# Two gated linear-attention blocks on one core: x tile 1 first on ScalarE's queue, its transposes behind tile 0's, A's keys of tile 2 before B's, gate column by a full-array matmul

## The chip, the cores and the metric

One core of one Trainium2 chip. The metric is the device time of one execution in microseconds (us), the slowest core's; with one core there is only one. Every execution also has a *span*: the profile's first program instruction to its last. The reported time is longer than the span.

## The reference

x is 2048 x 640, in bfloat16, with 32 heads of 20 columns. Two blocks, A and B, work on the same x with their own weights:

```
qkv = x @ wqkv;  phi(t) = where(t > 0, t + 1, exp(t)) + 1e-6
kv  = sum_s phi(k)[s] v[s]^T          (per head)
z   = sum_s phi(k)[s]
o   = (phi(q) @ kv) / (phi(q) . z + 1e-6)
out = o @ wo
g   = sigmoid((x * gate_w).sum(-1))
result = g * A + (1 - g) * B
```

## The kernel before

The program is recorded as operations, each with its engine, its inputs and outputs. A small scheduler orders them; on TensorE they stay in the order of recording. x is needed transposed (`XT`). Tiles 0 and 1 of x (128 rows each) are loaded plainly and transposed by TensorE against an identity; the other tiles come by transposing DMAs. The keys of a tile are five *key steps*, one per chunk of 128 rows of the weights; a step is a 128x512 and a 128x128 matmul. B's weights carry a 641st column, the gate's.

```python
    bgw = Buf("gw5")
    dma("ACT", "cst", CST[:, :], cap[:, :], 128 * CW * 2, outs=[bcst])
    ld_x("ACT", 1)
    dma("ACT", "gw", GW5[:, :], gate_w.rearrange("(c p) -> c p", p=128), 1280, outs=[bgw])
    for c in range(NC):
        if c == 0:
            ld_x("SP", c)
        ld_wk("SP", "A", c)
    for c in range(NC):
        ld_wk("SP", "B", c)
    for t0, t1 in ((2, 3), (3, 4), (4, 5), (5, 6), (6, 8), (8, 12), (12, 16)):
        xt_dma(t0, t1)
    ...                                                   # cut: the later loads
    def x_tp(t):                                          # cut: three groups of transposes
        ...                                               # each copied out of PSUM by VectorE
    def gate_col():                                       # gate_w as 5 rows of 128 -> a column
        op("PE", lambda e: e.transpose(tv(), GW5[:, :], IDN[0:NC, 0:NC]), 60.0, ...)
        op("DVE", lambda e: e.tensor_copy(WK["B"][:, :, D : D + 1], tv().unsqueeze(2)), ...)
    ...
    warm(4)                                               # warm-ups of 128x512
    warm(1, 2)
    pss = [Buf("k", "ps", 2) for _ in range(2)]
    x_tp(0)
    warm(6, 1)                                            # six warm-ups of 128x128
    k_step("A", 0, 0, pss[0])
    x_tp(1)
    k_step("A", 0, 1, pss[0])
    k_step("A", 1, 0, pss[1])
    k_step("A", 1, 1, pss[1])
    gate_col()
    for c in range(2, NC):
        for t in range(2):
            k_step("A", t, c, pss[t])
    for t in range(2):
        k_post("A", t, pss[t])
    pss = [Buf("k", "ps", 2) for _ in range(2)]
    for c in range(NC):
        for t in range(2):
            k_step("B", t, c, pss[t])                     # B's chunk serves two tiles
    for t in range(2):
        k_post("B", t, pss[t])
    for t in range(2, NT):
        for X in XS:
            k_unit(X, t)
    ...                                                   # cut: everything later, unchanged
```

Of the kernel before, what the change touches and what calls it, by code (L numbers as in the profile page):

```python
# [6 lines left out]
ACT = mybir.ActivationFunctionType  # L7
# [6 lines left out]
NT = 16  # L14
NB = 4
NC = 5
# [56 lines left out]
class Sched:  # L73
# [7 lines left out]
    def op(self, eng, fn, cost, ins=(), outs=(), after=(), prio=None, name="", dma=None):  # L81
        if eng == "ACT" and dma is None:
            after = list(after) + self.consts
        o = Op(eng, fn, cost, list(ins), list(outs), after, len(self.ops) if prio is None else prio, name, dma)
        self.ops.append(o)
        return o
# [171 lines left out]
def body(nc, A_x, A_wqkv, A_wo, B_x, B_wqkv, B_wo, gate_w, out, log=None):  # L258
# [7 lines left out]
    bf, f32 = dt.bfloat16, dt.float32  # L266
    sb = nc.alloc_sbuf_tensor
    XT = sb("XT", [128, NC, S], bf)
# [47 lines left out]
    TTR = sb("TTR", [128, NB, 4, 128], bf)  # L316
    FF = sb("FF", [128, NB, 512], bf)
    CST = sb("CST", [128, CW], bf)
    GW5 = sb("GW5", [NC, 128], bf)
    GE = sb("GE", [128, NT], f32)  # L320
    GG = sb("GG", [128, 2, NT], f32)
    ONE = sb("ONE", [128, 128], bf)
# [2 lines left out]
    PS = nc.alloc_psum_tensor("ps", [128, 8, 512], f32)  # L325


    IDN = sb("IDN", [128, 128], bf)
# [3 lines left out]
    op = sch.op  # L332
# [6 lines left out]
    def dma(q, name, dst, src, nbytes, ins=(), outs=(), after=(), issue=450.0, transpose=False, prio=None):  # L339
        def fn(e):  # L340
            d = dst() if callable(dst) else dst
            with nc.allow_non_contiguous_dma(reason="layout"):
                return e.dma_start(d, src() if callable(src) else src, transpose=transpose)

        o = op(q, fn, 0.0, ins, outs, after, prio=prio, name=name, dma=(issue, nbytes, 95.0 if transpose else 330.0))
        if loading:
            o.behind = chain.get(q)
            chain[q] = o
        return o
# [4 lines left out]
    def act_cost(n):  # L354
        return 190 + 0.833 * n

    def dve1(n):
        return 155 + 1.04 * n

    def dve4(n):  # L360
# [14 lines left out]
    bid = Buf("idn")  # L375
# [6 lines left out]
        ins=[bone],  # L382
        outs=[bid],
        name="idn",
    )
    bxo = Buf("xo")
    op("POOL", lambda e: e.memset(XN[:, :, D : D + 1], 1.0), 200.0, outs=[bxo], name="xones")

    def ld_x(q, t):
        dma(q, "x%d" % t, XN[:, t, 0:D], x[128 * t : 128 * t + 128, :], 163840, outs=[bxn[t]])  # L390

    def ld_wk(q, X, c, after=()):
        dma(q, "wk%s%d" % (X, c), WK[X][:, c, 0:D], wqkv[X][128 * c : 128 * c + 128, D : 2 * D], 163840, outs=[bwk[X, c]], after=after)

    def xt_dma(t0, t1):
        dma(
            "SP",
            "xt%d" % t0,
            XT[:, :, 128 * t0 : 128 * t1],
            x[128 * t0 : 128 * t1, :],  # L400
            (t1 - t0) * 163840,
            outs=bxt[t0:t1],
            issue=(t1 - t0) * 850.0,
            transpose=True,
        )
# [2 lines left out]
        return wqkv[X][:, k * D : k * D + D].rearrange("(c p) f -> p c f", p=128)  # L408

    bgw = Buf("gw5")  # L410
    dma("ACT", "cst", CST[:, :], cap[:, :], 128 * CW * 2, outs=[bcst])
    ld_x("ACT", 1)
    dma("ACT", "gw", GW5[:, :], gate_w.rearrange("(c p) -> c p", p=128), 1280, outs=[bgw])
    for c in range(NC):
        if c == 0:
            ld_x("SP", c)
        ld_wk("SP", "A", c)
    for c in range(NC):
        ld_wk("SP", "B", c)
    for t0, t1 in ((2, 3), (3, 4), (4, 5), (5, 6), (6, 8), (8, 12), (12, 16)):  # L420
        xt_dma(t0, t1)
    dma("SP", "xr", XN[:, 2:NT, 0:D], x[256:S, :].rearrange("(t p) d -> p t d", p=128), 14 * 163840, outs=bxn[2:])
    for X in XS:
# [14 lines left out]
    def warm(n, w=4):  # L438
        for i in range(n):
            op(  # L440
                "PE",
                lambda e: e.matmul(psw(bw, 128 * w), ONE[:, :], ONE[:, :].unsqueeze(1).to_broadcast([128, w, 128]), start=True, stop=True),  # L442
                107.0 * w,
                ins=[bone],
                outs=[bw],
                name="warm",
            )

    def x_tp(t):
        for lo, hi in ((0, 1), (1, 3), (3, 5)):  # L450
            bt = Buf("tp", "ps")
            for c in range(lo, hi):
                op(
                    "PE",
                    lambda e, c=c, lo=lo, bt=bt: e.matmul(  # L455
                        PS[:, bt.slot, 128 * (c - lo) : 128 * (c - lo) + 128],
                        XN[:, t, 128 * c : 128 * c + 128],
                        IDN[:, :],
                        start=True,
                        stop=True,  # L460
                    ),
                    100.0,
                    ins=[bxn[t], bid],
                    outs=[bt],
                    name="tp%d" % t,
                )
            half = Buf("xth")
            op(
                "DVE",
                lambda e, lo=lo, hi=hi, bt=bt: e.tensor_copy(  # L470
                    XT[:, lo:hi, 128 * t : 128 * t + 128],
                    PS[:, bt.slot, 0 : 128 * (hi - lo)].rearrange("p (c s) -> p c s", c=hi - lo),
                ),
                dve1(128 * (hi - lo)),
                ins=[bt],
                outs=[half],
                name="tpc%d" % t,
            )
            bxt[t].parts = getattr(bxt[t], "parts", []) + [half] * (hi - lo)
# [3 lines left out]
    def gate_col():  # L483
        bt = Buf("gwp", "ps")

        def tv():
            return PS[:, bt.slot, :].bitcast(bf)[:, 0:NC]

        op("PE", lambda e: e.transpose(tv(), GW5[:, :], IDN[0:NC, 0:NC]), 60.0, ins=[bgw, bid], outs=[bt], name="gwt")  # L489
        op(  # L490
            "DVE",
            lambda e: e.tensor_copy(WK["B"][:, :, D : D + 1], tv().unsqueeze(2)),
            170.0,
            ins=[bt],
            outs=[bgc],
            name="gwc",
        )
# [4 lines left out]
    def k_step(X, t, c, ps):  # L502
        w = D + 1 if X == "B" else D

        def fn(e):
            a = psw(ps, w)
            l = XT[:, c, 128 * t : 128 * t + 128]
            e.matmul(a[:, 0:512], l, WK[X][:, c, 0:512], start=(c == 0), stop=(c == NC - 1))  # L508
            return e.matmul(a[:, 512:w], l, WK[X][:, c, 512:w], start=(c == 0), stop=(c == NC - 1))  # L509

        xin = [bxt[t].parts[c] if hasattr(bxt[t], "parts") else bxt[t]]
        op(
            "PE",
            fn,
            mm_cost(512) + mm_cost(128),
            ins=xin + [bwk[X, c]] + ([bgc] if X == "B" else []),
            outs=[ps],
            name="k%s%d_%d" % (X, t, c),
        )
# [3 lines left out]
    def k_post(X, t, ps):  # L523
        ek = Buf("ek", "ek")
        ek2 = Buf("ek2")
        pk = Buf("pk%s%d" % (X, t))
        bpk[X, t] = pk
        first = []
        if X == "B":
            b = Buf("ge")  # L530
            bge.append(b)
            op(
                "ACT",
                lambda e: e.activation(GE[:, t : t + 1], psw(ps, D + 1)[:, D : D + 1], ACT.Exp, scale=-1.0),
                200.0,
                ins=[ps],
                outs=[b],
                name="ge",
            )
            first = [b]  # L540
        op("ACT", lambda e: e.activation(EK[:, ek.slot, :], psw(ps, D), ACT.Exp), act_cost(D), ins=[ps] + first, outs=[ek], name="ke")  # L541
        op(
            "DVE",
            lambda e: e.tensor_scalar(EK[:, ek.slot, :], EK[:, ek.slot, :], 1.0, EPS, op0=ALU.min, op1=ALU.add),  # L544
            dve4(D),
            ins=[ek],
            outs=[ek2],
            name="kt",
        )
        op(  # L550
            "DVE",
            lambda e: e.scalar_tensor_tensor(PKt[X][:, t, :], psw(ps, D), 0.0, EK[:, ek.slot, :], op0=ALU.max, op1=ALU.add),  # L552
            dve1(D),
            ins=[ps, ek, ek2],
            outs=[pk],
            name="ks",
        )

    def k_unit(X, t):
        ps = Buf("k", "ps", 2)  # L560
        for c in range(NC):
            k_step(X, t, c, ps)
        k_post(X, t, ps)
# [2 lines left out]
    warm(1, 2)  # L566
    pss = [Buf("k", "ps", 2) for _ in range(2)]
    x_tp(0)
    warm(6, 1)
    k_step("A", 0, 0, pss[0])  # L570
    x_tp(1)
    k_step("A", 0, 1, pss[0])
    k_step("A", 1, 0, pss[1])
    k_step("A", 1, 1, pss[1])
    gate_col()
    for c in range(2, NC):
        for t in range(2):
            k_step("A", t, c, pss[t])
    for t in range(2):
        k_post("A", t, pss[t])  # L580
    pss = [Buf("k", "ps", 2) for _ in range(2)]
    for c in range(NC):
        for t in range(2):
            k_step("B", t, c, pss[t])
    for t in range(2):
        k_post("B", t, pss[t])
    for t in range(2, NT):
        for X in XS:
            k_unit(X, t)

# [490 lines left out]
```

## Time and profile before

| | |
|---|---|
| median of the first 3 executions | 189.27 us (189.26 to 189.87) |
| profiled execution | 189.12 us, span 187.4 us |
| TensorE busy | 184.8 us |

The page of the kernel before: the span, the busy time of each engine (us, share of the span, instructions), and the chain of waits that ended last, by engine.

```profile
span 187.4 us, 3207 instructions
PE 184.8 (99%) x1266; PEld 108.4 (58%) x1266; DVE 136.0 (73%) x263; ACT 94.5 (50%) x168; POOL 0.6 (0%) x7
PE 99%; DVE 0%; issue 0%; DVEq 0%
```

TensorE is the bound: nearly the whole chain is its. Where its idle time lies, a table by stretches shows (start:end, length, then the busy time and instructions of TensorE, weight loads, VectorE, ScalarE and GpSimd, the granted clock, the DMA share, GB/s). The granted clock averages over recorded time alone, and the record starts at 4.37 us, so the 1.00 of the first line says nothing of the time before:

```profile
0.00:8.00 8.00, 7.56 (x46) 4.03 (x47) 2.27 (x8) 2.07 (x3) 0.59 (x7) 1.00 0.87 252
8.00:13.00 5.00, 5.00 (x39) 2.87 (x38) 4.00 (x8) 2.95 (x7) 0.00 (x0) 1.00 0.92 156
13.00:185.00 172.00, 172.00 (x1184) 101.37 (x1182) 129.44 (x247) 89.05 (x159) 0.00 (x0) 1.00 0.41 98
```

From 8 to 185 us TensorE is busy throughout, so inside the span only the head can move. (Busy times merge overlapping matmuls, so a short wait can hide in them; the distances between starts, below, are the finer measure.) The head, in TensorE's part of the timeline of the kernel before (start and length in us, instruction, `x` how many; `[idle before]`). The 128x128 halves of the key steps are left out here and in the later timelines, but for one; `...` stands for left-out lines:

```profile
2.51 0.69 PE L455 MATMUL ps<-IDN,XN 128*128 128x128 bf16 x5
2.99 0.84 PE L442 MATMUL ps<-ONE 128*128 128x128 bf16 x6
3.63 0.63 PE L508 MATMUL ps<-WKW,XT 128*128 128x512 bf16 x1
4.16 0.55 PE L455 MATMUL ps<-IDN,XN 128*128 128x128 bf16 x5
4.75 0.39 PE L508 MATMUL ps<-WKW,XT 128*128 128x512 bf16 x1
...
5.30 0.38 PE L508 MATMUL ps<-WKW,XT 128*128 128x512 bf16 x1
5.52 0.22 PE L509 MATMUL ps<-WKW,XT 128*128 128x128 bf16 x1
5.67 0.17 PE L489 MATMUL ps<-IDN,GW 5*128 5x5 bf16 x1
5.78 0.39 PE L508 MATMUL ps<-WKW,XT 128*128 128x512 bf16 x1
...
6.39 0.39 PE L508 MATMUL ps<-WKW,XT 128*128 128x512 bf16 x1
...
7.49 0.38 PE L508 MATMUL ps<-WKW,XT 128*128 128x512 bf16 x1
...
9.40 0.38 PE L508 MATMUL ps<-WKW,XT 128*128 128x512 bf16 x1
9.67 0.38 PE L508 MATMUL ps<-WKW,XT 128*128 128x512 bf16 x1
9.94 0.38 PE L508 MATMUL ps<-WKW,XT 128*128 128x512 bf16 x1
```

Lengths overlap here, since matmuls are pipelined (0.38 us long, 0.27 apart); read the distances between starts. L455 are the transposes, L442 the warm-ups, L508 the wide half of a key step. Two steps in the steady stream start 0.27 us apart. Across the gate's transpose (5.67) they are 5.30 and 5.78, 0.48 apart: that instruction costs 0.21 us. 7.49 is the eleventh key step, B's first; from there nothing waits.

### The profile page before, as it was taken

The numbers are of one execution on the slowest core, as the hardware profiler recorded it, in microseconds if no ns is written. First come the engines' busy times: TensorE is split into PE (matmuls) and PEld (weight loads), VectorE is DVE, ScalarE is ACT, GpSimd is POOL, SyncE is SP. The second block draws the span as 40 slices with busy tenths as digits, with TensorE's granted clock in tenths as the row PEclk, the third lists the DMA queues.
The fourth block names the chain that finished last, engine by engine and source line by source line (L and its number), as shares of the span: only waits on it lengthen the run. The fifth ranks groups of instructions, "written<-read, shape, count | busy, mean of one in ns | idle before, by whom it ended". The sixth has DMA issues, their size and how long they took to land.

```text
span 187.4 us, 3207 instructions
## 1 busy us (share of the span) xinstructions
PE 184.8 (99%) x1266; PEld 108.4 (58%) x1266; DVE 136.0 (73%) x263; ACT 94.5 (50%) x168; POOL 0.6 (0%) x7
## 2 busy tenths in 40 slices
PE   9999999999999999999999999999999999999995
PEld 5555555555566656655557556655566655555552
DVE  2489888878833546487798999879996999965600
ACT  3265655565554546644684667877624594100012
POOL 1000000000000000000000000000000000000000
PEclk9999999999999999999999999999999999999999
DMA  7989999999001011011501232540015365132322
GB/s 205 279 162 128 183 381 372 365 227 197 9 0 35 0 38 35 0 35 29 93 9 27 60 48 44 125 113 5 0 37 117 32 152 134 40 138 105 137 79 70
DMA packets 36301, 19.89 MB, mean 106 GB/s; under 512 B 25630, under 2 KB 36286, under 8 KB 36286
## 3 DMA queue, kind: packets, MB, share of 16 engines
q1 hardware_dynamic: 35844, 19.48, 42.9%
q8 instruction: 10, 0.16, 0.4%
q10 hardware_dynamic: 442, 0.20, 0.4%
q14 instruction: 5, 0.04, 0.1%
HBM read 9.39 MB, written 2.62 MB: 64 GB/s over the span
## 4 chain that ended last, share of the span: by engine, by line
PE 99%; DVE 0%; issue 0%; DVEq 0%
PE ps L903 23%; PE ps L743 23%; PE ps L508 19%; PE ps L617 18%; PE ps L618 5%; PE ps L509 5%; PE ps L659 2%; PE ps L442 1%; PE ps L697 1%; PE ps L455 1%; PE ps L698 0%; DVE TSB L947 0%; DVE ONE L372 0%; PE ps L489 0%; DVEq L230 0%
## 5 line engine op out<-in xcount | busy, mean ns | idle before, releaser
L508 PE MATMUL ps<-WKW,XT 128*128 128x512 bf16 x160 | 44.2, 381 | 0.0
L760 ACT ACTIVATE EK<-ps 128x512 bf16<-128x512 f32 x40 | 23.9, 598 | 31.6 <-PE ps L743 29.2
L509 PE MATMUL ps<-WKW,XT 128*128 128x128 bf16 (+1 forms) x160 | 35.2, 220 | 0.0
L541 ACT ACTIVATE EK<-ps 128x640 bf16<-128x640 f32 x32 | 22.3, 703 | 11.6 <-PE ps L509 5.7
L508 PEld LDWEIGHTS ps<-WKW,XT 128*128 128x128 bf16 x160 | 15.7, 98 | 18.9 <-DMA WKW<-in_A_wqkv_dram 0.4
L743 PE MATMUL ps<-XT,WQA 128*128 128x512 bf16 x100 | 24.5, 379 | 0.0
L743 PE MATMUL ps<-XT,WQB 128*128 128x512 bf16 x100 | 23.7, 379 | 0.0
L617 PE MATMUL ps<-XN,PKB 128*128 128x512 bf16 x80 | 23.5, 379 | 0.0
L617 PE MATMUL ps<-XN,PKA 128*128 128x512 bf16 x80 | 23.5, 379 | 0.0
L770 DVE TENSOR_SCALAR EK<-EK 128x512 bf16<-128x512 bf16 x40 | 11.6, 291 | 14.9 <-ACT EK L760 14.6
L618 PE MATMUL ps<-XN,PKA 128*128 128x129 bf16 x80 | 17.6, 220 | 0.0
L618 PE MATMUL ps<-XN,PKB 128*128 128x129 bf16 x80 | 17.6, 220 | 0.0
L903 PE MATMUL ps<-WPA,EX 128*128 128x512 bf16 x120 | 17.3, 299 | 0.0
L903 PE MATMUL ps<-WPB,PKA 128*128 128x512 bf16 x120 | 16.5, 299 | 0.0
L743 PEld LDWEIGHTS ps<-XT,WQB 128*128 128x128 bf16 x100 | 11.0, 118 | 8.5
L509 PEld LDWEIGHTS ps<-WKW,XT 128*128 128x128 bf16 x160 | 15.7, 98 | 0.0
L544 DVE TENSOR_SCALAR EK<-EK 128x640 bf16<-128x640 bf16 x32 | 10.4, 325 | 7.2 <-ACT EK L541 6.9
L743 PEld LDWEIGHTS ps<-XT,WQA 128*128 128x128 bf16 x100 | 10.7, 118 | 8.1
L617 PEld LDWEIGHTS ps<-XN,PKA 128*128 128x128 bf16 x80 | 9.4, 117 | 7.9
L617 PEld LDWEIGHTS ps<-XN,PKB 128*128 128x128 bf16 x80 | 9.4, 117 | 7.8
L949 ACT ACTIVATE TSB<-ps 128x640 bf16<-128x640 f32 (+1 forms) x3 | 2.0, 668 | 23.2 <-PE ps L903 23.2
L552 DVE SCALAR_TENSOR_TENSOR PKB<-ps,EK 128x640 bf16<-128x640 f32 x16 | 13.2, 825 | 0.6
(75 smaller groups left out, 240.6 us busy)
## 6 DMA issues: line engine op xcount, KB each, us to landing
out_dram<-TSB SPq DMA_DIRECT2D x15, 160.0 KB, 1.8
XN<-in_A_x_dram SPq DMA_DIRECT2D x1, 2240.0 KB, 8.8
WKW<-in_A_wqkv_dram SPq DMA_DIRECT2D x5, 160.0 KB, 4.1
WKW<-in_B_wqkv_dram SPq DMA_DIRECT2D x5, 160.0 KB, 4.3
WQA<-in_A_wqkv_dram SPq DMA_DIRECT2D x1, 800.0 KB, 10.5
WQB<-in_B_wqkv_dram SPq DMA_DIRECT2D x1, 800.0 KB, 13.2
WVA<-in_A_wqkv_dram SPq DMA_DIRECT2D x1, 800.0 KB, 12.7
WVB<-in_B_wqkv_dram SPq DMA_DIRECT2D x1, 800.0 KB, 14.2
```

The lines of the kernel that those rows point to most:

```text
L508: e.matmul(a[:, 0:512], l, WK[X][:, c, 0:512], start=(c == 0), stop=(c == NC - 1))
L509: return e.matmul(a[:, 512:w], l, WK[X][:, c, 512:w], start=(c == 0), stop=(c == NC - 1))
L541: op("ACT", lambda e: e.activation(EK[:, ek.slot, :], psw(ps, D), ACT.Exp), act_cost(D), ins=[ps] + first, outs=[ek], name="ke")
L544: lambda e: e.tensor_scalar(EK[:, ek.slot, :], EK[:, ek.slot, :], 1.0, EPS, op0=ALU.min, op1=ALU.add),
L552: lambda e: e.scalar_tensor_tensor(PKt[X][:, t, :], psw(ps, D), 0.0, EK[:, ek.slot, :], op0=ALU.max, op1=ALU.add),
L617: e.matmul(a[:, 0:512], l, XN[:, t, 0:512], start=(t == 0), stop=(t == NT - 1))
L618: return e.matmul(a[:, 512 : D + 1], l, XN[:, t, 512 : D + 1], start=(t == 0), stop=(t == NT - 1))
L659: r = e.matmul(PS[0:GR, ps.slot, GR * i : GR * i + GR], WV[X][:, c, lo : lo + GR], gv[:, c, :, lo // 5 : lo // 5 + 24], start=(c == 0), st ...
L743: r = e.matmul(PS[:, ps.slot, :], WQ[X][:, c, g::5], XT[:, c, 512 * b : 512 * b + 512], start=(c == 0), stop=(c == NC - 1),)
L760: lambda e: e.activation(EQ[:, eq.slot, :], PS[:, ps.slot, :], ACT.Exp),
L770: lambda e: e.tensor_scalar(EQ[:, eq.slot, :], EQ[:, eq.slot, :], 1.0, EPS, op0=ALU.min, op1=ALU.add),
L903: r = e.matmul(a[:, l0 - lo : h0 - lo], PQ[X, b][:, g, 128 * (t % 4) : 128 * (t % 4) + 128], WP[X][:, g, l0:h0], start=(X == first and g = ...
```

## The change

The intent is to have the first key steps earlier: tile 1's data is requested first on its queue, its transposes replace idle warm-ups, its copies go to the idle ScalarE. Using A's tile 2 before B gives B's weights more time. The gate's column is made by an ordinary matmul over all 128 rows (123 of them zero) instead of a transpose of 5 rows.

```diff
-    GW5 = sb("GW5", [NC, 128], bf)
+    GWZ = sb("GWZ", [128, 128], bf)
+    zgw = op("POOL", lambda e: e.memset(GWZ[:, :], 0.0), 200.0, name="zgw")
...
+    ld_x("ACT", 1)
+    dma("ACT", "gw", GWZ[0:NC, :], ..., after=[zgw])
     dma("ACT", "cst", CST[:, :], cap[:, :], 128 * CW * 2, outs=[bcst])
-    ld_x("ACT", 1)
-    dma("ACT", "gw", GW5[:, :], ...)
     for c in range(NC):
         if c == 0:
             ld_x("SP", c)
         ld_wk("SP", "A", c)
+    xt_dma(2, 3)
     for c in range(NC):
         ld_wk("SP", "B", c)
-    for t0, t1 in ((2, 3), (3, 4), ...):
+    for t0, t1 in ((3, 4), ...):
...
+                return e.activation(o, i, ACT.Copy) if t else e.tensor_copy(o, i)
-                "DVE",
+                "ACT" if t else "DVE",
...
-        op("PE", lambda e: e.transpose(tv(), GW5[:, :], IDN[0:NC, 0:NC]), 60.0, ...)
+        op("PE", lambda e: e.matmul(tv(), GWZ[:, :], IDN[:, 0:NC], start=True, stop=True), 60.0, ...)
...
     x_tp(0)
-    warm(6, 1)
-    k_step("A", 0, 0, pss[0])
+    warm(1, 1)
     x_tp(1)
-    k_step("A", 0, 1, pss[0])
-    k_step("A", 1, 0, pss[1])
-    k_step("A", 1, 1, pss[1])
+    for c in range(2):
+        for t in range(2):
+            k_step("A", t, c, pss[t])
     gate_col()
...
-    pss = [Buf("k", "ps", 2) for _ in range(2)]
-    for c in range(NC):
-        for t in range(2):
-            k_step("B", t, c, pss[t])
-    for t in range(2):
-        k_post("B", t, pss[t])
-    for t in range(2, NT):
+    k_unit("A", 2)
+    for t in range(3):
+        k_unit("B", t)
+    for t in range(3, NT):
         for X in XS:
             k_unit(X, t)
```

More of the change, by code (lines that the diff above doesn't have):

```diff
@@ L410, in body @@
     bgw = Buf("gw5")
+    ld_x("ACT", 1)
+    dma("ACT", "gw", GWZ[0:NC, :], gate_w.rearrange("(c p) -> c p", p=128), 1280, outs=[bgw], after=[zgw])
     dma("ACT", "cst", CST[:, :], cap[:, :], 128 * CW * 2, outs=[bcst])
-    ld_x("ACT", 1)
-    dma("ACT", "gw", GW5[:, :], gate_w.rearrange("(c p) -> c p", p=128), 1280, outs=[bgw])
     for c in range(NC):
@@ L417, in body @@
         ld_wk("SP", "A", c)
+    xt_dma(2, 3)
     for c in range(NC):
         ld_wk("SP", "B", c)
-    for t0, t1 in ((2, 3), (3, 4), (4, 5), (5, 6), (6, 8), (8, 12), (12, 16)):
+    for t0, t1 in ((3, 4), (4, 5), (5, 6), (6, 8), (8, 12), (12, 16)):
         xt_dma(t0, t1)
@@ L467, in x_tp, with copy @@
             half = Buf("xth")
-            op(
-                "DVE",
-                lambda e, lo=lo, hi=hi, bt=bt: e.tensor_copy(
-                    XT[:, lo:hi, 128 * t : 128 * t + 128],
-                    PS[:, bt.slot, 0 : 128 * (hi - lo)].rearrange("p (c s) -> p c s", c=hi - lo),
-                ),
-                dve1(128 * (hi - lo)),
+            def copy(e, lo=lo, hi=hi, bt=bt):
+                o = XT[:, lo:hi, 128 * t : 128 * t + 128]
+                i = PS[:, bt.slot, 0 : 128 * (hi - lo)].rearrange("p (c s) -> p c s", c=hi - lo)
+                return e.activation(o, i, ACT.Copy) if t else e.tensor_copy(o, i)
+            op(
+                "ACT" if t else "DVE",
+                copy,
+                act_cost(128 * (hi - lo)) if t else dve1(128 * (hi - lo)),
                 ins=[bt],
@@ L486, in tv @@
         def tv():
-            return PS[:, bt.slot, :].bitcast(bf)[:, 0:NC]
-        op("PE", lambda e: e.transpose(tv(), GW5[:, :], IDN[0:NC, 0:NC]), 60.0, ins=[bgw, bid], outs=[bt], name="gwt")
+            return PS[:, bt.slot, 0:NC]
+        op("PE", lambda e: e.matmul(tv(), GWZ[:, :], IDN[:, 0:NC], start=True, stop=True), 60.0, ins=[bgw, bid], outs=[bt], name="gwt")
         op(
```

## The prediction

> **What bounds the kernel now.** TensorE. The page's busy line gives PE 184.8 of 187.4 us, the chain of waits gives PE 99%. The idle rest is mostly the first 0.39 us and about 2.0 us after the last matmul. Nothing in the diff touches that tail, or TensorE's work after the first 13 us, where the timeline shows one key step (128x512 and 128x128) each 0.272 us without gaps. So only the head can move the time.
>
> **The head, before** (timeline and DMA landing records, us). Tile 0's transposes start at 2.51 (x tile 0 lands 2.37); six short warm-up matmuls follow; key step A0,0 starts at 3.63, at the half clock; tile 1's transposes at 4.16 (x tile 1 lands 3.67); the full clock is granted from 4.37. A's weight chunks 0 to 4 land at 3.22, 4.70, 5.50, 6.35, 6.82. Chunk 1 ends a wait before 4.75 and chunk 3 one before 6.39. The gate transpose costs 0.21 us (0.48 instead of 0.27 between two steps). From 6.39 there are no stalls; the eleventh key step (first of B) starts at 7.49.
>
> **What changes.** Removed: five warm-ups (0.107 us each, cold). Moved: tile 1's five transposes in front of A0,0, its three evacuations (0.95 us on VectorE) to ScalarE, which idles from 3.12 to 7.42; estimate 0.3 to 0.4 us each. The gate matmul should fall from 0.21 to about 0.05 us. By work alone, 0.4 us are won before chunk 2.
>
> But chunks 2 and 3 don't come sooner: the 16 engines are about saturated, the bytes ahead of chunk 3 are the same. The Trainium skill ("DMA: Bandwidth & Descriptors", Queues, rings and completion order) says that each DMA engine round-robins between queues; in this trace x tile 1's packets indeed interleave with SyncE's. Issued at 0.13 instead of 0.51, it should land near 2.8, but take share from x tile 0, which I expect at 2.4 to 2.7. A0,0 then starts at 3.6 to 3.8; A0,3 waits for chunk 3 at about 6.3. The gain shrinks to 0.05 to 0.15 us.
>
> **New risk.** The eleventh step is now A's tile 2. Its DMA transpose, queued behind chunk 4 (6.82), should land about 0.66 us later (as behind B's last chunk before): 7.48, needed at 7.40 to 7.45. A stall of 0 to 0.1 us eats most of the gain. B's chunks then land at about 7.9 to 9.6 (0.42 us apart, as before) and are needed at 8.85 to 9.94, now 0.27 instead of 0.54 us apart: enough, with 0.3 us of slack at the last.
>
> **Prediction: 189.15 us, range 188.7 to 189.8.** Faster by over 2%: 0.5%; same: 99%; slower: 0.5%.
>
> **Signs.** Right: PE still about 99%; A0,3 released by a DMA at 6.2 to 6.4; the gate step under 0.1 us; eleventh step at 7.35 to 7.55; nothing different later. Wrong: x tile 0 later than 2.8; a wait of over 0.2 us for tile 2's transpose or a B chunk; idle PE after 13 us.
>
> **What would make it wrong.** The skill ("TensorE: Matmul & The Clock Gate", Part 1) says the clock's activity window is free-running, so the granting moment (4.37 here) may shift between executions; one trace can't show it. If the new wait for x tile 0 leaves TensorE idle long enough to delay the full clock by a window (about 3.4 us by that page), up to 1 us is lost. If chunk 3 lands earlier, up to 0.4 us is gained.

## The result, and the profile after

| | before | after |
|---|---|---|
| median | 189.26 us (188.97 to 189.87, 6 runs) | 188.91 us (188.65 to 189.32, 6 runs) |
| profiled execution: time | 189.12 us | 188.96 us |
| profiled execution: span | 187.38 us | 187.58 us |
| time minus span | 1.74 us | 1.38 us |

The ratio of after to before is 0.9982, with a 95% interval of 0.9963 to 1.0001. A ratio is the mean time of one kernel's fast runs over that of the other's of the same rounds, so it is not quite the ratio of the medians.

The gain, about 0.35 us, fell within the predicted range. But the span of the profiled execution did not shrink; it grew by 0.2 us. The page of the changed kernel:

```profile
span 187.6 us, 3202 instructions
PE 184.6 (98%) x1261; PEld 107.9 (58%) x1261; DVE 135.4 (72%) x260; ACT 95.6 (51%) x171; POOL 0.8 (0%) x8
PE 96%; DMA 2%; SPq 0%; DVE 0%; issue 0%; DVEq 0%
```

The chain has 2% of DMA now. The stretches of the changed kernel, as above, show TensorE less busy in the first 8 us, and 37 instead of 39 matmuls in the next 5, though it is busy throughout:

```profile
0.00:8.00 8.00, 7.17 (x42) 3.77 (x43) 1.31 (x5) 3.08 (x7) 0.78 (x8) 1.00 0.86 222
8.00:13.00 5.00, 5.00 (x37) 2.56 (x35) 4.45 (x9) 3.03 (x6) 0.00 (x0) 1.00 0.92 195
13.00:185.00 172.00, 172.00 (x1182) 101.31 (x1180) 129.31 (x246) 88.92 (x158) 0.00 (x0) 1.00 0.39 99
```

The head in TensorE's timeline of the changed kernel (L457 are the transposes, L513 the wide half of a key step, L494 the gate):

```profile
2.64 0.69 PE L457 MATMUL ps<-IDN,XN 128*128 128x128 bf16 x5
3.12 0.31 PE L444 MATMUL ps<-ONE 128*128 128x128 bf16 x1
3.23 0.74 PE L457 MATMUL ps<-IDN,XN 128*128 128x128 bf16 x5
3.76 0.63 PE L513 MATMUL ps<-WKW,XT 128*128 128x512 bf16 x1
4.30 0.44 PE L513 MATMUL ps<-WKW,XT 128*128 128x512 bf16 x1
5.09 0.39 PE L513 MATMUL ps<-WKW,XT 128*128 128x512 bf16 x1 [0.30 <-DMA WKW<-in_A_wqkv_dram]
5.37 0.38 PE L513 MATMUL ps<-WKW,XT 128*128 128x512 bf16 x1
5.64 0.17 PE L494 MATMUL ps<-IDN,GWZ 128*128 128x5 bf16 x1
5.70 0.39 PE L513 MATMUL ps<-WKW,XT 128*128 128x512 bf16 x1
...
7.39 0.39 PE L513 MATMUL ps<-WKW,XT 128*128 128x512 bf16 x1
...
9.30 0.38 PE L513 MATMUL ps<-WKW,XT 128*128 128x512 bf16 x1
9.70 0.39 PE L513 MATMUL ps<-WKW,XT 128*128 128x512 bf16 x1
10.12 0.39 PE L513 MATMUL ps<-WKW,XT 128*128 128x512 bf16 x1
```

TensorE does two key steps by 4.6 us instead of one and a set of transposes, and then has 0.30 us with nothing to do: chunk 1 of A's weights landed at 5.04 us, against 4.70 before. The gate now costs at most 0.06 us (5.37 to 5.70, less 0.27); chunk 2 landed at 5.66, which alone would have held the step at 5.70. The eleventh step starts at 7.39, 0.10 ahead. But then the steps at 9.70 and 10.12 are 0.40 and 0.42 apart instead of 0.27. The waits of the changed kernel between 4 and 11 us (who, for whom, us in total, times, longest) say for what:

```profile
PEld ps L513 <- DMA WKW<-in_A_wqkv_dram: 0.6, 1, 0.6
PEld ps L513 <- DMA WKW<-in_B_wqkv_dram: 0.6, 2, 0.3
PEld ps L513 <- DMA XT<-in_A_x_dram: 0.2, 1, 0.2
```

B's last two chunks landed at 9.65 and 10.08 us; 0.28 us are lost (0.40 + 0.42 - 2 x 0.27). The sum, 0.10 won and 0.28 lost, is the span's growth by 0.2.

So this pair of traces has the gain neither in the head nor anywhere else inside the span. It is in what follows. Behind the span's end the trace still has records of semaphores: one that all engines count up in turn, then resets of all the others, then the first one again. Offsets from the span's end, in us:

```
             first exchange                    second exchange
before  0.120 0.164 0.202 0.237 0.283   1.072 1.107 1.145 1.189 1.212   1.663 1.702 1.736 1.782
after   0.119 0.163 0.201 0.235 0.282   1.074 1.108 1.147 1.191 1.214   1.312 1.350 1.384 1.431
```

Everything agrees within 0.003 us up to the fifth count of the second exchange. Then the next one comes 0.451 us later before, 0.098 us after. The reported time ends about 0.05 us before the last of these records in both kernels (189.12 against 187.385 + 1.782; 188.96 against 187.576 + 1.431). The Trainium skill ("Runtime: NRT & Kernel Launch", "The ~15µs preamble/postamble breakdown") describes such stages behind a kernel: a barrier, a reset of semaphores, a barrier again. For the barrier in front of a kernel it gives the pass of one semaphore through five engines as about 355 ns. The second exchange behind the changed kernel takes as long, 0.357 us from 1.074 to 1.431; that behind the kernel before takes 0.710.

Which part of the change shortens it, and is the head really no better, or was the first pair of traces unlucky? That is what the experiments are for.

### The profile page after: what moved, and what is told of

It reads as the page before. It is cut to its first block, busy times and chain, and to the rows that moved or that the text cites. A ratio compares the mean times of both kernels' runs of the same rounds, so it can differ in the third digit from the quotient of the medians.

```text
span 187.6 us, 3202 instructions
## 1 busy us (share of the span) xinstructions
PE 184.6 (98%) x1261; PEld 107.9 (58%) x1261; DVE 135.4 (72%) x260; ACT 95.6 (51%) x171; POOL 0.8 (0%) x8
## 4 chain that ended last, share of the span: by engine, by line
PE 96%; DMA 2%; SPq 0%; DVE 0%; issue 0%; DVEq 0%
PE ps L904 23%; PE ps L744 23%; PE ps L513 18%; PE ps L618 18%; PE ps L619 5%; PE ps L514 5%; DMA WKW<-in_A_wqkv_dram 2%; PE ps L660 2%; PE ps L698 1%; SPq L343 0%; PE ps L699 0%; DVE TSB L948 0%; DVEq L230 0%; PE ps L494 0%
## 5 line engine op out<-in xcount | busy, mean ns | idle before, releaser
L513 PE MATMUL ps<-WKW,XT 128*128 128x512 bf16 x160 | 44.4, 381 | 0.3 <-DMA WKW<-in_A_wqkv_dram 0.3
L513 PEld LDWEIGHTS ps<-WKW,XT 128*128 128x128 bf16 x160 | 15.7, 98 | 19.8 <-DMA WKW<-in_A_wqkv_dram 0.6
L557 DVE SCALAR_TENSOR_TENSOR PKA<-ps,EK 128x640 bf16<-128x640 f32 x16 | 13.2, 825 | 0.6
```

What stands on the lines that cost most here:

```text
L513: e.matmul(a[:, 0:512], l, WK[X][:, c, 0:512], start=(c == 0), stop=(c == NC - 1))
L557: lambda e: e.scalar_tensor_tensor(PKt[X][:, t, :], psw(ps, D), 0.0, EK[:, ek.slot, :], op0=ALU.max, op1=ALU.add),
```

## The experiments

Twelve experiments ran, e1 with the changed kernel itself, all with correct results. "Last gap" is the gap just shown (0.451 and 0.098 us). The mean inside the span is worked out: mean time less the "time minus span" of the same kernel's profiled execution. Each execution's own span is on record too, to 0.1 us, for all but the first six executions of before; the means of these spans agree with this column within 0.05 us. Instruction counts are those in the trace, waits included. The kernel before stands with all its 50 executions.

| run | mean time, us (n) | time minus span | last gap | mean inside | ScalarE / VectorE instructions | ratio (95%) |
|---|---|---|---|---|---|---|
| before | 189.28 (50) | 1.74 | 0.451 | 187.54 | 231 / 312 | |
| after | 188.94 (6) | 1.38 | 0.098 | 187.56 | 238 / 309 | 0.9982 (0.9963 to 1.0001) |
| e1 again | 188.92 (5) | 1.38 | 0.099 | 187.54 | 238 / 309 | 0.9976 (0.9951 to 1.0001) |
| e2 no A2 first | 188.85 (6) | 1.38 | 0.098 | 187.47 | 236 / 309 | 0.9972 (0.9950 to 0.9995) |
| e3 A2 only | 189.50 (6) | 1.72 | 0.458 | 187.78 | 233 / 312 | 1.0007 (0.9984 to 1.0029) |
| e4 A2, then B in pairs | 189.25 (6) | 1.38 | 0.099 | 187.87 | 234 / 309 | 0.9997 (0.9955 to 1.0039) |
| e5 gate only | 188.92 (6) | 1.74 | 0.451 | 187.18 | 231 / 312 | 0.9979 (0.9956 to 1.0003) |
| e6 old gate | 189.11 (6) | 1.36 | 0.098 | 187.75 | 238 / 309 | 0.9987 (0.9964 to 1.0010) |
| e7 one warm-up only | 189.15 (4) | 1.75 | 0.475 | 187.40 | 233 / 312 | 0.9989 (0.9961 to 1.0018) |
| e8 x tile 1 first only | 189.31 (4) | 1.74 | 0.456 | 187.57 | 231 / 312 | 0.9998 (0.9969 to 1.0028) |
| e9 ScalarE plus 7 | 189.10 (6) | 1.74 | 0.451 | 187.36 | 238 / 312 | 0.9998 (0.9969 to 1.0026) |
| e10 VectorE plus 3 | 189.14 (1) | 1.73 | 0.449 | | 238 / 312 | one look |
| e11 for both ends | 188.58 (6) | 1.36 | 0.098 | 187.22 | 236 / 309 | 0.9967 (0.9946 to 0.9989) |
| e12 three copies moved | 189.19 (6) | 1.37 | 0.098 | 187.82 | 232 / 309 | 0.9999 (0.9981 to 1.0016) |

Two columns behave very differently. The last gap takes two values, 0.45 to 0.48 and 0.10, and nothing between. That is one trace of each kernel, but the single executions say the same: time minus span is 1.68 to 1.85 us in all 71 with a span on record of the kernels with the long gap, and 1.32 to 1.48 in all 41 fast ones of those with the short gap. The mean inside the span is noisy: the heads of before, e9 and e12 do the same critical work, and yet their means are 187.54, 187.36 and 187.82. So a difference of 0.2 us inside the span, between means of six, proves nothing here.

The traces show where that noise arises. In all thirteen fast ones TensorE's last matmul starts 177.57 to 177.59 us after the eleventh key step, once the waits in the ten or so steps behind it are taken off (0.28 us in after and e4, 0.50 in e10, 0.08 in e3, 0.12 in e7, none elsewhere). The eleventh step itself starts anywhere from 6.96 to 8.03 us. Inside the span these kernels differ by their heads and those waits alone.

### e1: the changed kernel again

No edit.

> The changed kernel as it is, to have its span and its time beside those of the kernel before on one chip. In the first pair of traces the change lengthened the span (187.4 to 187.6 us) while the reported time fell (189.12 to 188.96), so the part outside the span fell from 1.72 to 1.36 us. Theory OUTSIDE: the 0.34 us gain lies outside the span; then spans are equal within 0.2 us on the average and time minus span is 0.3 us smaller with the change. Rival HEAD: TensorE's head is what gains, and the first trace of before was a lucky one; then the mean span falls by 0.2 to 0.4 us and time minus span is the same for both within 0.1 us. Both expect a ratio of 0.997 to 0.999.

Measured: ratio 0.9976; time minus span 1.38 us. With the first six, eleven executions of the changed kernel have a mean of 188.93 us, and of 187.55 inside the span, against 187.54 for 50 of the kernel before. OUTSIDE holds: the whole gain, 0.35 us, lies behind the span; HEAD, which wanted a shorter span, falls.

One execution of the six, the profiled one, took 1110.25 us. It is left out of the mean. Its page, span, busy times and the largest group of matmuls:

```profile
span 1108.9 us, 3202 instructions
PE 1106.5 (100%) x1261; PEld 395.1 (36%) x1261; DVE 139.3 (13%) x260; ACT 97.8 (9%) x171; POOL 0.8 (0%) x8
L513 PE MATMUL ps<-WKW,XT 128*128 128x512 bf16 x160 | 261.2, 1705 | 0.0
```

A 128x512 matmul took 1705 ns on the average instead of 381, in the whole execution, while VectorE's and ScalarE's busy times grew only by 3% and 2%. Only TensorE was slow. Its closing exchange was as short as after's (0.099), which shows that the end doesn't depend on how the body ran. No granted clock is on record for this execution, but six fast traces have none either. No later execution repeated this, and its cause stays open.

### e2: the change without A's tile 2 first

```diff
-    xt_dma(2, 3)
     for c in range(NC):
         ld_wk("SP", "B", c)
-    for t0, t1 in ((3, 4), ...
+    for t0, t1 in ((2, 3), (3, 4), ...
-    k_unit("A", 2)
-    for t in range(3):
-        k_unit("B", t)
+    (B's tiles 0 and 1 in pairs, as before)
```

> The change with its third part undone: B's weight chunks are issued and used before A's tile 2, in pairs of tiles, as before. HEAD: TensorE no longer waits for tile 2's transpose (0.05 us) nor for B's chunks 3 and 4 (0.13 and 0.15 us), so the ratio to the kernel before is 0.996 to 0.998, 0.2 to 0.4 us faster than the changed kernel. OUTSIDE: whatever shortens the part outside the span is not in this part; same ratio as e1 within 0.001 apart from those waits. If instead the third part is where the gain comes from, the ratio is 1.000 or above.

Measured: ratio 0.9972, mean 0.08 us under after's, last gap 0.098. The waits for tile 2 and B's chunks are gone from the trace, but 0.08 us is within the noise. The third part of the change is not where the gain comes from.

### e3: only A's tile 2 first

```diff
+    xt_dma(2, 3)                    (before B's chunks)
+    k_unit("A", 2); then B's tiles 0 to 2, each alone
```

> The kernel before with only the third part: A's keys of tile 2 before B's, its transpose issued before B's chunks. HEAD: the waits for B's chunks (about 0.3 us in the changed kernel's trace) come in and nothing is won, so a ratio of 1.000 to 1.002. OUTSIDE: 1.000 to 1.002, and time minus span as in the kernel before. If the third part is the source of the gain: 0.997 to 0.999.

Measured: ratio 1.0007, last gap 0.458. No gain, as both theories expected. Here B's weights cost one short wait (steps at 9.72 and 10.07, 0.35 apart, so 0.08), not 0.3 us.

### e4: A's tile 2, then B in pairs

```diff
     k_unit("A", 2)
-    for t in range(3):
-        k_unit("B", t)
+    (B's tiles 0 and 1 in pairs, chunk by chunk)
+    k_unit("B", 2)
```

> The changed kernel, but after A's tile 2 B's tiles 0 and 1 are taken together, chunk by chunk, so that each chunk of B's weights is used for 0.54 us instead of 0.27 before the next one is needed. HEAD: the waits for B's chunks 3 and 4 (0.28 us together) go; ratio to before 0.996 to 0.998, 0.2 to 0.3 us faster than e1. OUTSIDE: the same gain beside e1, for this is inside the span; time minus span as in e1.

Measured: ratio 0.9997 with one execution at 190.97 us; the median is 189.06. The waits for B's chunks are gone as expected, and a new one stands in their place, as the weight loads in the timeline of e4 show:

```profile
9.26 0.10 PEld L513 LDWEIGHTS ps<-WKW,XT 128*128 128x128 bf16 x1 [0.44 <-DVE PKA L557]
```

Five accumulators of two PSUM banks each are wanted at that moment, and there are eight banks: B's second tile waits until VectorE has taken tile 0's keys out (ends 9.20). The expected gain was turned into a wait for PSUM. This did not beat the change.

### e5 and e6: the gate alone, and all but the gate

e5 is the kernel before with:

```diff
-        op("PE", lambda e: e.transpose(tv(), GW5[:, :], IDN[0:NC, 0:NC]), ...)
+        op("PE", lambda e: e.matmul(tv(), GWZ[:, :], IDN[:, 0:NC], start=True, stop=True), ...)
+    (GWZ zeroed by GpSimd, gate_w loaded to its first 5 rows)
```

> The kernel before with only the fourth part: the gate column by a full-array matmul instead of the transpose of 5 rows. The traces so far show, behind the span's end, the closing exchange of one semaphore among the engines: its last gap is 0.45 us in the kernel before and in e3, 0.10 us in the changed kernel, e1, e2 and e4. Theory GATE: the transpose of 5 rows leaves TensorE something to put back at the end, so this run's last gap is 0.10 us, time minus span about 1.38 us (1.73 before), ratio 0.997 to 0.999. Rival COUNT: the number of TensorE's instructions (1266 before, 1261 after) sets it, by how the last ones are fetched; then 0.45 us, time minus span 1.73 and a ratio of 0.999 to 1.001. Rival QUEUE: the order of ScalarE's transfers sets it; also 0.45 us.

e6 is the changed kernel with the same lines reversed.

> The changed kernel with the old gate transpose of 5 rows put back, all else as changed. GATE: last gap of the closing exchange 0.45 us, time minus span 1.73 us, ratio to before 0.999 to 1.002 (all of the gain gone, and the gate step back at 0.2 us). COUNT and QUEUE: last gap 0.10 us, time minus span 1.38, ratio 0.997 to 0.999.

Measured: e5 has the long gap (0.451) and e6 the short one (0.098), the opposite of what GATE wanted. The gate has nothing to do with the end; that theory, mine, falls. Inside the span the gate's own cost is well shown: the distance of the two key steps around the old gate, in each trace where the full clock is already granted and no chunk is late, is 0.47 to 0.48 us (before, e3, e7, e8, e9, e12), so 0.20 us for the gate; the new one costs 0.03 in e11, the one trace with it that meets both conditions (after's 0.06 has the late chunk 2 in it). The means agree in sign (e5 0.36 us under before inside the span, e6 0.19 over after), at the edge of the noise. Whether it is the transposing mode, the use of 5 rows or the bfloat16 output (float32 in the new form) that costs this was not separated.

e6 shows the other lottery of the head. TensorE's timeline of e6:

```profile
3.75 0.63 PE L512 MATMUL ps<-WKW,XT 128*128 128x512 bf16 x1
4.28 0.63 PE L512 MATMUL ps<-WKW,XT 128*128 128x512 bf16 x1
4.81 0.63 PE L512 MATMUL ps<-WKW,XT 128*128 128x512 bf16 x1
5.35 0.63 PE L512 MATMUL ps<-WKW,XT 128*128 128x512 bf16 x1
6.14 0.61 PE L512 MATMUL ps<-WKW,XT 128*128 128x512 bf16 x1
6.64 0.40 PE L512 MATMUL ps<-WKW,XT 128*128 128x512 bf16 x1
6.94 0.38 PE L512 MATMUL ps<-WKW,XT 128*128 128x512 bf16 x1
```

The first four steps start 0.53 us apart, and the one at 6.14 is still followed only after 0.50: the half clock, until after 6.1 us. In the trace of before the full clock was granted at 4.37 us.

### e7 and e8: one warm-up only, and x tile 1 first only

```diff
-    warm(6, 1)                                    (e7)
+    warm(1, 1)
```

> The kernel before with one short warm-up matmul instead of six between the first transposes and the first key step: TensorE's count falls to 1261 as in the changed kernel. COUNT: last gap 0.10 us, time minus span 1.38 us, ratio 0.997 to 0.999. GATE and QUEUE: 0.45 us, 1.73 us and 0.999 to 1.001; chunk 1 lands at 4.7 to 5.0 us and TensorE waits longer for it, so the head gains nothing from the removal of 0.5 us of work.

```diff
+    ld_x("ACT", 1)                                (e8)
     dma("ACT", "cst", ...)
-    ld_x("ACT", 1)
```

> The kernel before with only x tile 1 ahead of the small constant on ScalarE's queue. QUEUE: last gap 0.10 us and time minus span 1.38. GATE and COUNT: 0.45 us and 1.73. In the head: x tile 1 lands near 3.1 instead of 3.67 us, x tile 0 about 0.1 us later (2.5), and since the first transposes of tile 1 still stand behind a key step, the eleventh key step starts at 7.4 to 7.6 as before; ratio 0.999 to 1.001.

Measured: both have the long gap (0.475 and 0.456), so neither the number of TensorE's instructions (1261 matmuls in e7, as after) nor the order of ScalarE's transfers sets it. COUNT in its TensorE form and QUEUE fall. In the head of e7 the full clock was granted at 3.13 us, the earliest of all, and chunk 1 landed at 4.10, so its eleventh step came at 6.96; my expectation of a later chunk was wrong there. In e8 x tile 1 landed at 2.92, chunk 1 at 5.02, the clock came at 5.15 and the eleventh step at 7.75, later than expected.

Over all traces but e1's slow one, chunk 1 landed at 4.30 to 5.04 us (mean 4.70, six traces) with x tile 1 first on its queue, and at 3.89 to 4.72 (mean 4.29, seven traces) with it second. The ranges overlap. It fits what the Trainium skill says ("DMA: Bandwidth & Descriptors", "Queues, rings and completion order"), that a DMA engine alternates between queues that have work: in the trace of after, ScalarE's queue moved 118 KB between 1.75 and 2.25 us and SyncE's 62 KB. That what is brought forward on one queue is taken from the other fits these numbers; with ranges that overlap it is not shown.

### e9 and e10: useless instructions on one engine

Left as candidates were the three copies as such, ScalarE's instruction count (234 and more had the short gap), and VectorE's (312 long, 309 short). e9 adds to the kernel before:

```diff
+    for j in range(7):
+        op("ACT", lambda e, j=j: e.activation(IDL[:, j : j + 1], EPSC[:, :], ACT.Exp), ...)
```

> The kernel before with seven useless activations of one column, each to a column of its own, right behind the activation table's load, where ScalarE has nothing to do until 7.4 us: ScalarE's program then has 238 instructions, as in the changed kernel (231 before), and nothing else differs. Every kernel so far with the short last gap (0.10 us) has 234 to 238 instructions on ScalarE and 309 on VectorE; every one with the long gap (0.45) has 231 to 233 and 312. Theory ACT-COUNT: last gap 0.10 us, time minus span 1.38 us, ratio 0.997 to 0.999, although only work was added. Rival DVE-COUNT: VectorE's 312 instructions set it, so the gap stays 0.45 us, time minus span 1.73 us, ratio 0.999 to 1.001. If what matters is what the change does (tile 1's copies on ScalarE as such), also 0.45 us.

e10 adds to the changed kernel:

```diff
+    for j in range(3):
+        op("DVE", lambda e, j=j: e.memset(IDL[:, j : j + 1], 0.0), ...)
```

> The changed kernel with three useless one-column memsets on VectorE in its first microsecond: 312 instructions on VectorE, as in the kernel before, 238 on ScalarE, as in the changed kernel. DVE-COUNT: last gap of the closing exchange 0.45 us, time minus span 1.73 us. ACT-COUNT, or the copies as such: 0.10 us and 1.38 us. One look; the time itself is one draw from 188.6 to 189.4.

Measured: e9 keeps the long gap (0.451, with 238 instructions on ScalarE). e10 turns the short gap into the long one (0.449, time minus span 1.73 us) by three memsets that end in the first microsecond. e10 has one execution only, but in no kernel did any execution cross from one value to the other. ScalarE's count is out, and so are tile 1's copies on ScalarE, which e10 still has. VectorE's count is in.

### e11: a version for both ends

The kernel before with the new gate, `warm(1, 1)` and tile 1's copies on ScalarE; x tile 1 second on its queue, B's tiles in pairs.

> A version for both ends: the kernel before with the full-array gate matmul, one short warm-up instead of six, and tile 1's copies on ScalarE (236 and 309 instructions), but x tile 1 still second on its queue and B's tiles in pairs before A's tile 2. ScalarE's first transfer being x tile 1 put chunk 1 of A's weights at 4.6 to 5.0 us (five runs) against 3.9 to 4.7 without it (four runs), and A's tile 2 first cost waits of 0.05 to 0.5 us for B's chunks. HEAD: eleventh key step at 6.9 to 7.3 us, unless the full clock is granted later than 5 us; with the short last gap the mean time is 188.4 to 188.8 us, ratio 0.9955 to 0.998. If the head's gain is only the draw of the clock's moment, 188.9 as in the changed kernel, ratio 0.998.

Measured: median 188.56 us (188.44 to 188.72), ratio 0.9967 (0.9946 to 0.9989): 0.35 us under the changed kernel's median and the only one whose six executions all lie below the median of the changed kernel. The last gap is 0.098. TensorE's timeline of e11 at the gate and at the eleventh key step:

```profile
5.25 0.38 PE L512 MATMUL ps<-WKW,XT 128*128 128x512 bf16 x1
5.53 0.17 PE L493 MATMUL ps<-IDN,GWZ 128*128 128x5 bf16 x1
5.55 0.38 PE L512 MATMUL ps<-WKW,XT 128*128 128x512 bf16 x1
...
7.18 0.38 PE L512 MATMUL ps<-WKW,XT 128*128 128x512 bf16 x1
```

The eleventh step at 7.18 and no later wait. Of the ratio, 0.0019 is the end's 0.35 us. The rest, about 0.25 us against the runs of before on the same chip, is the head; the interval of e11 overlaps those of after and e1, so how much of that rest is the draw of a good head is not settled.

### e12: VectorE's count by another route

Nothing of the change; three 128x1 copies go to ScalarE, which leaves 309 instructions on VectorE. In the trace they start 124 to 140 us into the kernel, not at about 80 as I expected.

```diff
+        zin = (X, g) in (("B", 2), ("B", 3), ("B", 4))
         op(
-            "DVE",
+            "ACT" if zin else "DVE",
...                                            # cut: the operation in either form
```

> The kernel before with nothing of the change, but three tiny copies of 128x1 (the key sums of B's last three groups, about 80 us into the kernel) moved from VectorE to ScalarE: 309 instructions on VectorE, as in the changed kernel, 232 on ScalarE, 1296 for TensorE as before. Theory DVE-COUNT: the last gap of the closing exchange is 0.10 us, time minus span 1.38 us, and the mean time falls by 0.2 to 0.5 us (0.35 from the end, the head being the lottery that it is in the kernel before): ratio 0.9975 to 0.999. Rival COPIES: tile 1's copies on ScalarE, or anything else in the head of the changed kernel, set it and e10 fell for another reason; then 0.45 us, 1.73 us and 0.999 to 1.001.

Measured: the last gap is 0.098 us and time minus span 1.37: the end became short with nothing in the head changed. So VectorE's instruction count is what sets the gap, shown in both directions (e10 and e12). But the mean time did not fall: ratio 0.9999 (0.9981 to 1.0016), against 0.9975 to 0.999 expected. That expectation was missed. The mean inside the span was 0.28 us above that of the 50 executions of before, with the same head. The trace of e12 shows that the copies are not to blame in the profiled execution. Its last matmul starts at 185.28 us, against 185.07 before, but its eleventh key step was already as late, 7.70 against 7.49:

```profile
7.70 0.38 PE L508 MATMUL ps<-WKW,XT 128*128 128x512 bf16 x1
```

From there to the last matmul both kernels take 177.57 to 177.58 us, so the moved copies cost TensorE nothing there, and the 0.21 us are the head's. Of the other five executions only times and spans are on record; that their heads were late too is likely, but not shown.

## Why the prediction was right, and where it was not

The time, 188.91 us, lies in the predicted range of 188.7 to 189.8, and within 2% as expected. The gain is three times the expected 0.1 us, and it has another source. That the number was right is luck: the gain foreseen in the head cannot be told from zero, and one that was not foreseen came from behind the span. The range was wide enough to hold no gain at all (189.28).

- *"Nothing in the diff touches that tail ... So only the head can move the time."* This step failed. The diff takes three instructions from VectorE, and the engines' closing exchange behind the span then takes 0.35 us less (last gap 0.098 instead of 0.451); e10 and e12 show that these three are enough, either way. I had looked at the end of the span and not behind it, though the table had 1.7 us there.
- *"The gain shrinks to 0.05 to 0.15 us"* in the head. Measured inside the span: 187.55 (11 executions) against 187.54 (50), so -0.01 us, give or take 0.1. That error is one standard error of the difference, rounded up, from the scatter of single executions, 0.23 and 0.37 us. The head gained nothing that can be told from zero.
- *Gate "from 0.21 to about 0.05"*: right, 0.03 (e11), at most 0.06 (after).
- *"A0,3 waits for chunk 3 at about 6.3"*: wrong in its cause. It started at 6.26 without a wait, because chunks 1 and 2 were later (5.04 and 5.66) and made everything queue behind them, and chunk 3 came earlier (6.08).
- *x tile 1 "near 2.8", x tile 0 "2.4 to 2.7"*: 3.13 and 2.50.
- *Tile 2's transpose at 7.48, a stall of 0 to 0.1*: landed 7.34; the step was 0.05 us late. Right.
- *B's chunks at 7.9 to 9.6, "enough"*: wrong. They landed at 8.29 to 10.08 and cost 0.28 us in the profiled execution, 0.08 in e3's and 0.5 in e10's. I had carried over the distance of 0.42 us between plain transfers. Behind the transposing transfer of tile 2 the first B chunk landed 0.95 us later (0.64 to 1.40 in the five fast traces with this order). SyncE also issued that chunk 1.36 us after the transposing transfer (2.81 and 4.17), where plain ones are issued about 0.47 apart; whether the issue or the transfer delays it was not separated.
- *"The granting moment may shift between executions"*: right, and a part of the scatter. The records have 3.13 (e7), 3.15 (e9), 3.86 (e10), 4.13 (e5), 4.37 (before), 4.41 (after) and 5.15 us (e8); in e6 it was later than 6.1. The Trainium skill ("TensorE: Matmul & The Clock Gate", Part 1) has a free-running window of 3413 ns; a spread of 3 us fits it. The eleventh key step goes with it in part: 6.96 in e7, 8.03 in e6. The landing of the chunks counts too: e9, with the clock at 3.15, had its eleventh step at 7.22, since chunk 3 landed only at 6.07.

Left open: why the count of VectorE's instructions matters. The Trainium skill ("Runtime: NRT & Kernel Launch", "Instruction fetch mechanics") says that each engine's program is fetched in blocks, ahead of its use, and a block's border that falls into the closing sequence would be a natural cause. No run shows it: the last recorded fetch is at 179.5 us before and 179.9 after, and no transfer is recorded in the closing exchange. Only 309 and 312 were tried, so neither the border nor whether it repeats is known, nor whether the count itself matters or something that goes with it, such as the length of VectorE's program.

## What to carry to other kernels

When a change of 0.2% is to be explained, split the reported time into the span and what lies outside it before explaining anything inside: here the whole difference was behind the last instruction, and three useless memsets on one engine could undo it. Compare heads over several executions, since the clock's grant and the landing of the first loads move it by more than the change did. Where the first transfers keep the DMA engines busy (87% in the first 8 us here), pulling one of them forward may delay another: chunk 1 landed 0.4 us later on the average with x tile 1 in front, though the ranges overlap. Taking away work that has a cost of its own, as the gate's 0.2 us, has no such price.

## What the Trainium skill lacked or had wrong

- "Runtime: NRT & Kernel Launch" gives one time for each closing barrier. Here the second exchange takes 0.36 us, as the page has it for the pass through five engines in front of a kernel, or 0.71 us, and of all counts in the traces only VectorE's goes with it: 309 (short, the changed kernel and five others) or 312 (long, the kernel before and six others). No page says that an instruction count can move the end.
- "TensorE: Matmul & The Clock Gate", Part 1, puts the transition at about 4 us, with a variation of 500 ns. Matmuls started at 0.39 us in every trace, and the full clock came between 3.13 us and later than 6.1 us; the page's free-running window of 3413 ns fits that spread of 3 us better than its 500 ns.
- The same page tells of a clock seen stuck low for over 50 us. Here one execution of about 120 ran TensorE slow from end to end: 1110.25 us, 1705 ns instead of 381 for a 128x512 matmul. No granted clock was recorded, but none was in six fast traces either.
- No page has the cost of a small transpose between two full matmuls: 0.20 us with 5 rows, against 0.03 us (e11) for a full-array matmul with 5 columns. It would belong to "TensorEngine Tiling (Array Packing)", Key Properties, which names a drain at a change of tiling mode but gives no time.
- "DMA: Bandwidth & Descriptors" doesn't tell what a change from a transposing transfer to plain ones costs on one queue: the plain transfer behind it landed 0.64 to 1.40 us later (five fast traces), where in the changed kernel plain ones follow each other at 0.42 to 0.48 us.
